# Chunk-selected attention feeding a soft mixture of experts: load order, score groups, slot steps and output halves rearranged in one change

## The chip, the cores and the metric

The kernel runs on one core of one Trainium2 chip. The metric is the time of one execution on the device in microseconds. The core has five engines that run their own instruction streams in program order: TensorE (PE in the profile, with its weight loads as PEld), VectorE (DVE), ScalarE (ACT), GpSimd (POOL) and SyncE (SP). Engines wait for each other through semaphores. Here GpSimd issues all loads and SyncE all stores.

## What is computed

The first part is attention in which every query sees only the six best chunks of 32 keys, chosen by an upper bound of the scores; the second part is a soft mixture of experts on the attention's output.

```python
# attention: B, H, S, D = 4, 8, 768, 64; chunk = 32, so 24 chunks; top_k = 6
k_min, k_max = k_chunks.min(axis=3), k_chunks.max(axis=3)
ub = sum over d of max(q * k_min, q * k_max)          # one bound per query and chunk
ub = where(causal by chunk, ub, -1e9)
top_chunks = argsort(ub)[..., -6:]
scores = q @ k.T / 8, kept where the chunk is selected and the key is not later
x = softmax(scores) @ v                               # to [3072, 512]

# soft MoE: 8 experts with 4 slots each, D = 512, F = 1024
logits = x @ phi
d = softmax of logits over the 3072 rows              # dispatch
slot_input = d.T @ x
slot_out[e] = relu(slot_input[e] @ w1[e]) @ w2[e]
c = softmax of logits over the 32 slots               # combine
out = c @ slot_out                                    # float32 [3072, 512]
```

Inputs come in float32 and are cast to bf16 by the load itself.

## The kernel before

The 32 heads are worked on in 16 pairs; the two heads of a pair share the 128 partitions, 64 each. The order of all work is written out by hand: a loop over slots `i` (lines 479 to 566) has for each slot a list of steps of different pairs, so that every engine finds work. In slot `i` these belong to pair `i`: `scores` and `expo` for six groups; to pair `i + 1`: the upper bound (`ubound`), the choice of chunks (`select`) and its transposes (`ns_transposes`, `evac_ns`); to pair `i + 2`: the transposes of k and q (`transposes`, `evac_T`), the chunk minima and maxima (`kmin`, `kmax`) and the split of q in its negative and positive part (`qsplit`); to pair `i - 1`: the product with v (`pv`); to pair `i - 2`: `normalise` and the transposes of x. The head is slots -2 and -1 of the same loop.

Scores are kept transposed (keys in partitions, queries along the row). A group is a list of pieces `(key block, first query offset, width, column)`; the causal triangle of 6 x 6 blocks of 128 is packed into six groups (line 30), three 512 and three 384 wide, for two heads at a time. Each piece costs two matmuls of keys against queries (line 270, one for each head) and two or four that add the mask of chunks which were not selected (line 280). ScalarE takes the exponential of a whole group (line 293), then GpSimd zeroes the upper triangle of the diagonal block (line 295). PSUM tiles come from three pools: `p_sc` (two, scores), `p_at` (one) and `p_tp` (two, everything else). A step whose tile isn't free yet makes TensorE wait, and with it all that stands behind on TensorE.

The mixture of experts runs batch by batch in slots behind the attention of that batch (`moe(step, i - 3)` does a step for the batch whose last pair is `i - 3`): `moe_logits`, `moe_copy`, `moe_max`, `moe_bound`, `moe_exp`, `moe_exp2`, `moe_scale`, `moe_comb`, `moe_comb2`, `moe_dispatch`, `moe_ct`. A running maximum lets the sums over rows be rescaled. The last batch is worked on behind the loop.

Loads go through one queue, in the order in which GpSimd issues them: k and q of pair `i + 4` (line 129) and v of pair `i + 2` (line 134), 192 KB each, and the sixteen expert weights (line 122), 1024 KB each, `w_sb[0..7]` for w1 and `w_sb[8..15]` for w2. `wplan` says how many weights a slot issues. Before, weight 0 is issued in the head, weight 1 in slot -1, and one in each slot from 2 to 15. Slots below 14 issue them behind `load_v`, slots 14 and 15 at their top.

Behind the loop come the last batch's dispatch, the first expert layer (`experts_in`, line 670, reads `w_sb[0..7]`), the second (`experts_out`, line 710) and the output. Experts are worked on in two groups `g` of four, four column tiles of TensorE at a time; `experts_out` for `g = 1` reads `w_sb[12..15]`, all four within the first four matmuls:

```python
def experts_out(f, gs, ys):
    for y, g in ((y, g) for y in ys for g in gs):
        for fg in range(f * 4, (f + 1) * 4):
            for j in range(4):
                e = g * 4 + j
                nc.tensor.matmul(so_ps[y][j * CH:(j + 1) * CH, :], lhsT=hT_pad[:, fg, e, :],
                    rhs=w_sb[E + e][:, fg * Dm + y * HD:fg * Dm + (y + 1) * HD], ...)
```

The output is 24 blocks of 128 rows, two to a store (line 761), scaled by VectorE and ScalarE by turns (lines 754 and 756). `keep(n)` issues n matmuls whose result isn't used.

Of the kernel before, what the change touches and what calls it, by code (L numbers as in the profile page):

```python
# [30 lines left out]
    [(0, 0, 384, 0)],  # L31
    [(1, 0, 256, 0), (0, 384, 128, 256)],
    [(2, 0, 512, 0)],
    [(5, 0, 128, 0), (1, 256, 384, 128)],
    [(3, 0, 384, 0)],
    [(4, 0, 256, 0), (0, 512, 256, 256)],
]
WIDTH = [sum(p[2] for p in g) for g in GROUPS]
BLOCK = {}
for _g, _pieces in enumerate(GROUPS):  # L40
    for _kg, _q0, _w, _c in _pieces:
        for _x in range(0, _w, P):
            BLOCK[(_kg, _kg + (_q0 + _x) // P)] = (_g, _c + _x)


@with_exitstack
def kernel(
# [41 lines left out]
    w_sb = []  # L89
    for i in range(EARLY):  # L90
        w_sb.append(static.tile([P, NDG * F], BF16, name=f"w_sb{i}"))
# [47 lines left out]

    load(0, "k")  # L140
    load(0, "q")
    make_identity(nc, ident)
    load(1, "k")
    load(1, "q")
    for t in (caus, qgrp, headsel, squad, ns_t[0], ns_t[1], c_pad):
        nc.vector.memset(t, 0.0)
    nc.vector.memset(ones_sq, 1.0)
    for t in v_t:
        nc.vector.memset(t[:, :, :, D:D + 1], 1.0)
    for h in range(2):  # L150
        nc.vector.memset(headsel[h * 64:(h + 1) * 64, :, h, :], 1.0)

    nc.gpsimd.affine_select(
# [9 lines left out]
    load_w(0)  # L163
    nc.gpsimd.affine_select(
        out=squad, in_=squad, compare_op=ALU.not_equal, fill=NEG, base=0,
        pattern=[[-CH, 2], [-64, 2], [-1, NCHUNK]], channel_multiplier=1,
    )
    nc.gpsimd.affine_select(
        out=squad, in_=squad, compare_op=ALU.not_equal, fill=-1.0, base=-NCHUNK,
        pattern=[[-CH, 2], [-64, 2], [0, NCHUNK]], channel_multiplier=1,  # L170
    )
    load_v(0)
    load_v(1)
# [38 lines left out]
    def qsplit(i):  # L212
        qT = st["qT", i]
        t = tpu.tile([P, 2, S], BF16, name="qpn", tag="qpn")
        nc.vector.tensor_scalar_min(t[:, 0, :], qT, 0.0)
        nc.vector.tensor_scalar_max(t[:, 1, :], qT, 0.0)  # L216
        st["qpn", i] = t
# [45 lines left out]
    def scores(i, g):  # L263
        ps = p_sc.tile([P, 2, 512], F32, name="sc_ps", tag="sc")
        kT, qT, nsT = st["kT", i], st["qT", i], st["nsT", i]
        for kg, q0, w, c in GROUPS[g]:
            qs = slice(kg * P + q0, kg * P + q0 + w)
            for h in range(2):
                r = slice(h * 64, (h + 1) * 64)
                nc.tensor.matmul(  # L270
                    ps[:, h, c:c + w], lhsT=kT[r, kg * P:(kg + 1) * P], rhs=qT[r, qs],
                    start=True, stop=False,
                )
            t0, t1 = kg + q0 // P, kg + (q0 + w) // P
            runs = [(x, max(t0, x * NJ), min(t1, (x + 1) * NJ)) for x in range(2)]
            runs = [r for r in runs if r[1] < r[2]]
            for x, f, l in runs:
                for h in range(2):
                    r = slice(h * 64, (h + 1) * 64)
                    nc.tensor.matmul(  # L280
                        ps[:, h, c + (f - t0) * P:c + (l - t0) * P],
                        lhsT=smask[r, x, kg].rearrange("p a b -> p (a b)"),
                        rhs=nsT[r, (f - x * NJ) * P:(l - x * NJ) * P], start=False, stop=(l == t1),
                    )
        st["scps", i, g] = ps

    def expo(i, g):
        w = WIDTH[g]
        if w == 512:
            e = ep.tile([P, 2, 512], BF16, name="e_sb", tag="e_sb")  # L290
        else:
            e = ep3.tile([P, 2, 384], BF16, name="e3_sb", tag="e3_sb")
        nc.scalar.activation(e[:, :, :w], st.pop(("scps", i, g))[:, :, :w], func=ACT.Exp, scale=scale)  # L293

        nc.gpsimd.affine_select(  # L295
            out=e[:, :, :P], in_=e[:, :, :P], compare_op=ALU.is_ge, fill=0.0,
            base=0, pattern=[[0, 2], [1, P]], channel_multiplier=-1,
        )
        st["e", i, g] = e

    def pv(i, ts):
# [7 lines left out]
        for t in ts:  # L309
            for h in range(2):  # L310
                o = at[:, h, (t - tb) * (D + 1):(t - tb + 1) * (D + 1)]
                for kg in range(t + 1):
                    g, c = BLOCK[(kg, t)]
# [68 lines left out]
    def moe_exp(b):  # L382
        lg = st["lg", b]
# [32 lines left out]
    def moe_comb(b):  # L416

        lg = st.pop(("lg", b))
# [31 lines left out]
    def moe_ct(b):  # L450
# [5 lines left out]
        nc.vector.tensor_copy(cT_all[:, b * NQT:(b + 1) * NQT, :], ps)  # L456
# [11 lines left out]
    wplan = {i: 1 for i in range(-1, NPAIR)}  # L468
    for i in (0, 1):
        wplan[i] = 0  # L470
# [8 lines left out]
    for i in range(-2, NPAIR):  # L479
# [4 lines left out]
        if have(i):  # L484
            scores(i, 0)
            expo(i, 0)
            scores(i, 1)
            expo(i, 1)
        moe(moe_max, i - 3)
        if have(i + 1):  # L490
            ubound(i + 1)
        if have(i - 2):
            normalise(i - 2)
        moe(moe_bound, i - 3)
        if have(i + 1):
            select(i + 1)
        if i == -1:
            nc.gpsimd.dma_start(out=phi_sb, in_=moe_phi.rearrange("(hg p) s -> p hg s", p=P))
            make_identity(nc, identf)
# [3 lines left out]
        if i == -1:  # L503
            ns_transposes(0)
            evac_ns(0)
        if have(i + 4) and i >= -1:
# [4 lines left out]
        moe(moe_exp, i - 3)  # L511
        if have(i):
# [4 lines left out]
        moe(moe_exp2, i - 3)  # L517
# [4 lines left out]
        if have(i + 2):  # L522
            transposes(i + 2, "q")
            evac_T(i + 2, "q")
            kmin(i + 2)
        if have(i - 2):
            evac_x(i - 2)
        if have(i + 2):
            kmax(i + 2)
        moe(moe_scale, i - 3)  # L530
        moe(moe_comb, i - 3)
        if have(i + 2) and i >= 0:
# [3 lines left out]
        if have(i):  # L536
            scores(i, 4)
            expo(i, 4)
            if i == LAST:
                pv(i - 1, [5])  # L540
            scores(i, 5)
            expo(i, 5)
        moe(moe_comb2, i - 3)
        if have(i + 1) and i >= 0:
            ns_transposes(i + 1)
            evac_ns(i + 1)
# [3 lines left out]
        if have(i - 1) and i < LAST:  # L550
            pv(i - 1, [5])
        if have(i + 2):
            qsplit(i + 2)
        if i == -2:
            nc.vector.tensor_tensor(schunk[:, :, :, 0], squad[:, :, 0, :], squad[:, :, 1, :], op=ALU.add)
            nc.scalar.copy(
                smask.rearrange("p o t a x -> p (o t a) x"),
                schunk.rearrange("p o c x -> p (o c) x").broadcast_to([P, 2 * NCHUNK, CH]),
            )
# [52 lines left out]
    keep(2)  # L612
# [12 lines left out]
    nc.vector.tensor_reduce(rm, lg1, axis=AX.X, op=ALU.max)  # L625
    dm = small.tile([P, 1, NS], F32, name="dm", tag="dm")
# [13 lines left out]
    op = ctx.enter_context(tc.tile_pool(name="op", bufs=5))  # L640
# [17 lines left out]
    cinv = tail.tile([P, B * NQT], F32, name="cinv")  # L658
    zinv = tail.tile([P, 1], F32, name="zinv")
# [28 lines left out]
    def zsum():  # L688
        ps = p_tp.tile([P, 1], F32, name="z_ps", tag="tp")
        nc.tensor.matmul(  # L690
            ps, lhsT=zrow.rearrange("p j s -> p (j s)"), rhs=identf[:1, :1], start=True, stop=True)
        nc.vector.reciprocal(zinv, ps)

    def csums():
        ps = p_tp.tile([P, B * NQT], F32, name="cs_ps", tag="tp")
        for n in range(B * NQT):
            nc.tensor.matmul(
                ps[:, n:n + 1], lhsT=cT[:, n // 2, n % 2], rhs=ones_sq[:, :1], start=True, stop=True)
        nc.vector.reciprocal(cinv, ps)

    HD = Dm // 2
    so_t = p_at.tile([P, 2, 512], F32, name="so_ps", tag="at")
    so_ps = [so_t[:, y, :HD] for y in range(2)]
# [20 lines left out]
    experts_out(0, [0], [0, 1])  # L724
    hidden_T(1)
    zsum()
    experts_out(0, [1], [0, 1])
    experts_out(1, [0, 1], [0])
    nc.scalar.activation(so_sb[0], so_ps[0], func=ACT.Copy, scale=zinv)
    experts_out(1, [0, 1], [1])  # L730
    nc.scalar.activation(so_sb[1], so_ps[1], func=ACT.Copy, scale=zinv)
    csums()


    homes = ((p_sc, "sc"), (p_tp, "tp"), (p_sc, "sc"), (p_tp, "tp"), (p_at, "at"))
    n = 0
    for m in range(B * NQT // 2):
        o_sb = op.tile([P, 2, Dm], F32, name="o_sb", tag="o_sb")
        rows = out[m * 2 * P:(m + 1) * 2 * P, :].rearrange("(p x) d -> p x d", x=2)
        for x in range(2):  # L740
            pool, tag = homes[n % 5]
            if n == 0:
                o_ps = pool.tile([P, 2, Dm], F32, name="o2_ps", tag=tag)
                halves = [o_ps[:, y, :HD] for y in range(2)]
            else:
                o_ps = pool.tile([P, Dm], F32, name="o_ps", tag=tag)
                halves = [o_ps[:, y * HD:(y + 1) * HD] for y in range(2)]
            for y in range(2):
                nc.tensor.matmul(halves[y], lhsT=cT[:, m, x], rhs=so_sb[y], start=True, stop=True)  # L749
            if n == 0:  # L750
                for y in range(2):
                    nc.vector.tensor_scalar_mul(o_sb[:, x, y * HD:(y + 1) * HD], halves[y], cinv[:, n:n + 1])
            elif x == 0:
                nc.vector.tensor_scalar_mul(o_sb[:, x, :], o_ps, cinv[:, n:n + 1])
            else:
                nc.scalar.activation(o_sb[:, x, :], o_ps, func=ACT.Copy, scale=cinv[:, n:n + 1])  # L756
            n += 1
            if m in (0, B * NQT // 2 - 1):
                nc.sync.dma_start(out=rows[:, x], in_=o_sb[:, x, :])
        if m not in (0, B * NQT // 2 - 1):  # L760
            nc.sync.dma_start(out=rows, in_=o_sb)
# [30 lines left out]
```

## Time and profile before

| what | value |
|---|---|
| median of three runs | 171.62 us (171.58 to 172.8) |
| the profiled execution | 172.21 us |
| its span, first to last instruction | 170.5 us |
| TensorE busy | 137.8 us (81%) |
| TensorE weight loads busy | 99.3 us (58%) |
| VectorE busy | 121.5 us (71%) |
| ScalarE busy | 122.6 us (72%) |
| GpSimd busy | 104.0 us (61%) |
| loads written by the software queue | 26.25 MB |
| stores by the hardware queue | 6.29 MB |
| first exponential of slot 0 | at 14.20 us |
| first exponential of slot 13 | at 110.79 us |
| first store issued | at 151.73 us |

The profile shows one execution. Its rows count from the first instruction; a time of day such as "at 110.79" is on that scale. Busy time is the union of an engine's instructions; TensorE's matmuls overlap and their ends are modelled, so its busy time says less than that of the others. The execution takes 1.7 us more than the span. In the 40 slices each slice is 4.26 us long, and its digits are tenths.

### The profile page before, as it was taken

The numbers are of one execution on the slowest core, as the hardware profiler recorded it, in microseconds if no ns is written. First come the engines' busy times: TensorE is split into PE (matmuls) and PEld (weight loads), VectorE is DVE, ScalarE is ACT, GpSimd is POOL, SyncE is SP. The second block draws the span as 40 slices with busy tenths as digits, with TensorE's granted clock in tenths as the row PEclk, the third lists the DMA queues.
The fourth block names the chain that finished last, engine by engine and source line by source line (L and its number), as shares of the span: only waits on it lengthen the run. The fifth ranks groups of instructions, "written<-read, shape, count | busy, mean of one in ns | idle before, by whom it ended". The sixth has DMA issues, their size and how long they took to land.

```text
span 170.5 us, 6183 instructions
## 1 busy us (share of the span) xinstructions
PE 137.8 (81%) x2574; PEld 99.3 (58%) x2575; DVE 121.5 (71%) x416; ACT 122.6 (72%) x166; POOL 104.0 (61%) x202
## 2 busy tenths in 40 slices
PE   0458988999999898999999899979889989896300
PEld 0335555777666767766776667657566855763200
DVE  3468768999999976999997798988742651166510
ACT  3355999999999877999987799978777522175510
POOL 7977759788878777888878878547663800000000
PEclk9999999999999999999999999999999999999965
DMA  3999999999999999999999999999999980029995
GB/s 46 163 156 185 182 212 188 129 152 184 184 214 190 211 197 209 193 211 195 212 197 205 196 207 202 203 203 200 202 208 212 215 163 13 4 76 407 404 400 195
DMA packets 40460, 32.94 MB, mean 193 GB/s; under 512 B 26352, under 2 KB 34544, under 8 KB 40432
## 3 DMA queue, kind: packets, MB, share of 16 engines
q0 software_dynamic: 38416, 26.25, 104.2%
q1 hardware_dynamic: 2016, 6.29, 9.4%
q8 instruction: 20, 0.33, 0.7%
q14 instruction: 8, 0.07, 0.1%
HBM read 52.49 MB, written 6.29 MB: 345 GB/s over the span
## 4 chain that ended last, share of the span: by engine, by line
PE 39%; ACT 21%; DVE 15%; DMA 14%; issue 5%; POOL 2%; DVEq 0%; ACTq 0%; POOLq 0%
ACT e_sb L293 15%; DMA k_in<-in_k_dram 10%; PE sc_ps L270 7%; PE at_ps L314 5%; PE tr_ps L181 5%; PE sc_ps L280 5%; DMA out_dram<-o_sb 4%; DVE x_sb L327 3%; PE h_ps L670 2%; PE so_ps L710 2%; DVE qpn L216 2%; PE ub_ps L229 2%; DVE mx L241 2%; ACT qT L190 2%; PE xT_ps L336 2%
## 5 line engine op out<-in xcount | busy, mean ns | idle before, releaser
L293 ACT ACTIVATE e_sb<-sc_ps 128x768 bf16<-128x768 f32 (+1 forms) x96 | 82.9, 930 | 9.7 <-PE sc_ps L280 9.7
L295 POOL TENSOR_SCALAR_AFFINE_SELECT e_sb<-e_sb 128x256 bf16<-128x256 bf16 x96 | 38.7, 413 | 19.6 <-ACT e_sb L293 18.9
L270 PE MATMUL sc_ps<-qT,kT 64*128 64x384 bf16 (+3 forms) x288 | 40.3, 299 | 4.2 <-ACT e_sb L293 4.1
L280 PE MATMUL sc_ps<-nsT,smask 64*128 64x384 bf16 (+2 forms) x320 | 38.6, 281 | 0.0
L314 PE MATMUL at_ps<-v_t,e_sb 128*128 128x65 bf16 x672 | 29.8, 194 | 1.5 <-DVE x_sb L327 1.2
L314 PEld LDWEIGHTS <-e_sb 128*128 128x128 bf16 x672 | 25.3, 98 | 3.9 <-DVE x_sb L327 1.2
L270 PEld LDWEIGHTS <-kT 64*128 64x128 bf16 x288 | 17.0, 95 | 15.5 <-issue 10.4
L241 DVE MAX8 mx<-ub_ps 128x8 f32<-128x8 f32 (+1 forms) x192 | 16.9, 161 | 3.6 <-PE ub_ps L229 2.0
L280 PEld LDWEIGHTS <-smask 64*128 64x128 bf16 x320 | 16.6, 96 | 3.8 <-issue 0.6
L199 DVE TENSOR_REDUCE mm<-kT 128x24 bf16<-128x768 bf16 x16 | 15.1, 945 | 4.6 <-ACT kT L190 4.5
L190 ACT COPY kT<-tr_ps 128x768 bf16<-128x768 bf16 x16 | 12.8, 799 | 7.5 <-PE tr_ps L181 6.7
L134 POOL DMA_DIRECT2D v_t<-in_v_dram x16 | 16.7, 1045 | 2.0 <-PE ns_ps L252 1.4
L327 DVE TENSOR_TENSOR x_sb<-at_ps,inv 128x768 bf16<-128x768 f32 (+1 forms) x17 | 15.5, 911 | 0.6
L205 DVE TENSOR_REDUCE mm<-kT 128x24 bf16<-128x768 bf16 x16 | 15.1, 943 | 0.0
L181 PE MATMUL tr_ps<-ident,k_in 128*64 128x128 bf16 x192 | 9.4, 240 | 6.3 <-DMA k_in<-in_k_dram 5.5
L190 ACT COPY qT<-tr_ps 128x768 bf16<-128x768 bf16 x16 | 12.9, 805 | 2.0 <-PE tr_ps L181 2.0
L129 POOL DMA_DIRECT2D k_in<-in_k_dram x16 | 11.7, 729 | 1.5 <-POOLq L776 0.8
L122 POOL DMA_DIRECT2D w_sb<-in_moe_w_dram x16 | 11.4, 710 | 1.5 <-DMA w_sb<-in_moe_w_dram 1.5
L756 ACT ACTIVATE o_sb<-o_ps,cinv 128x512 f32<-128x512 f32 x12 | 8.1, 686 | 4.9 <-PE o_ps L749 2.4
L129 POOL DMA_DIRECT2D q_in<-in_q_dram x16 | 11.5, 720 | 0.0
L216 DVE TENSOR_SCALAR qpn<-qT 128x768 bf16<-128x768 bf16 x16 | 11.0, 685 | 0.0
L347 DVE COPY xT_sb<-xT_ps 128x768 bf16<-128x768 bf16 (+1 forms) x15 | 8.1, 540 | 4.0 <-PE xT_ps L336 3.9
(116 smaller groups left out, 196.5 us busy)
## 6 DMA issues: line engine op xcount, KB each, us to landing
w_sb<-in_moe_w_dram POOLq DMA_DIRECT2D x16, 1024.0 KB, 14.4
out_dram<-o_sb SPq DMA_DIRECT2D x10, 512.0 KB, 4.9
k_in<-in_k_dram POOLq DMA_DIRECT2D x16, 192.0 KB, 9.7
q_in<-in_q_dram POOLq DMA_DIRECT2D x16, 192.0 KB, 10.0
v_t<-in_v_dram POOLq DMA_DIRECT2D x16, 192.0 KB, 10.8
out_dram<-o_sb SPq DMA_DIRECT2D x4, 256.0 KB, 3.4
phi_sb<-in_moe_phi_dram POOLq DMA_DIRECT2D x1, 32.0 KB, 9.0
```

What stands on the lines that cost most here:

```text
L129: nc.gpsimd.dma_start(out=t, in_=src.rearrange("h (p g) d -> p h (g d)", p=P))
L134: nc.gpsimd.dma_start(out=v_t[i % NV][:, :, :, :D], in_=v[b, 2 * j:2 * j + 2].rearrange("h (g p) d -> p h g d", p=P),)
L181: nc.tensor.matmul(ps[h * 64:(h + 1) * 64, g, :], lhsT=src[:, h, g * D:(g + 1) * D], rhs=ident, is_transpose=True,)
L190: nc.scalar.copy(t.rearrange("d (p g) -> d p g", g=NQT), st.pop((nm + "ps", i)).rearrange("d g p -> d p g"),)
L199: nc.vector.tensor_reduce(mm[:, 0, 0, :], kT, axis=AX.X, op=ALU.min)
L241: nc.vector.max(mx[:, a, :], ub[:, a, :max(8, 4 * t + 4)])
L270: nc.tensor.matmul(ps[:, h, c:c + w], lhsT=kT[r, kg * P:(kg + 1) * P], rhs=qT[r, qs], start=True, stop=False,)
L280: nc.tensor.matmul(ps[:, h, c + (f - t0) * P:c + (l - t0) * P], lhsT=smask[r, x, kg].rearrange("p a b -> p (a b)"), rhs=nsT[r, (f - x * NJ ...
L293: nc.scalar.activation(e[:, :, :w], st.pop(("scps", i, g))[:, :, :w], func=ACT.Exp, scale=scale)
L295: nc.gpsimd.affine_select(out=e[:, :, :P], in_=e[:, :, :P], compare_op=ALU.is_ge, fill=0.0, base=0, pattern=[[0, 2], [1, P]], channel_mult ...
L314: nc.tensor.matmul(o, lhsT=st["e", i, g][:, h, c:c + P], rhs=v_t[i % NV][:, h, kg, :], start=(kg == 0), stop=(kg == t),)
L327: nc.vector.tensor_tensor(st["x", b][:, t0:t1, 2 * j:2 * j + 2, :].rearrange("p t h d -> p h t d"), at[:, :, :, :D], inv.broadcast_to([P, ...
```

## The change

It has seven parts.

1. `GROUPS`: the two groups with 512 columns stand first, the pieces of key blocks 0 and 1 are dealt differently (eight pieces instead of nine), and the last pair has an order of its own, `GROUPS_LAST`. `expo` masks each piece that begins on the diagonal; there are six such blocks as before, with two in group 4 and none in group 5.
2. The head is written out ahead of the loop: eight matmuls on `ones_sq` into an unused tile first, then the first k; one, three and four more of them later. The mask tile `smask` is built first, the second k is transposed ahead of the first `ubound`, the positive part of the first q is taken by ScalarE, and weight 0 is issued last.
3. In slots 0 and 1 four groups are done in a row.
4. In each slot the MoE steps move: `moe_max` between groups 0 and 1, `moe_bound` ahead of `normalise`, `moe_comb` behind `select`, `moe_exp` behind groups 2 and 3, `moe_exp2` behind the q transposes; the copy of batch 2's combine weights moves to the last slot.
5. `wplan`: one weight in slots 2, 4, 5, 6, 8, 9, 10 and 12, two in 13, three in 14 and two in 15. The first eight weight tiles have a pool of their own that is closed ahead of the output, whose tiles take the room.
6. The column sums of the first three batches move ahead of the last batch's dispatch, where two spare matmuls stood; those of the last one join the row sum in `sums`.
7. The second expert layer is done one column half at a time, and the first six output blocks are computed, scaled and stored by halves.

```diff
 GROUPS = [
-    [(0, 0, 384, 0)],
-    [(1, 0, 256, 0), (0, 384, 128, 256)],
     [(2, 0, 512, 0)],
     [(5, 0, 128, 0), (1, 256, 384, 128)],
+    [(0, 0, 384, 0)],
     [(3, 0, 384, 0)],
-    [(4, 0, 256, 0), (0, 512, 256, 256)],
+    [(4, 0, 256, 0), (1, 0, 256, 256)],
+    [(0, 384, 384, 0)],
 ]
+GROUPS_LAST = [
+    [(0, 0, 512, 0)],
+    [(1, 0, 512, 0)],
+    [(2, 0, 384, 0)],
+    [(4, 0, 256, 0), (2, 384, 128, 256)],
+    [(3, 0, 384, 0), (1, 512, 128, 384)],
+    [(5, 0, 128, 0), (0, 512, 256, 128)],
+]
...
+    def warm(n):
+        r = ones_sq.rearrange("p (o c) -> p o c", o=1).broadcast_to([P, 4, P])
+        for _ in range(n):
+            nc.tensor.matmul(warm_ps, lhsT=ones_sq, rhs=r, start=True, stop=True)
...
-        nc.vector.tensor_scalar_max(t[:, 1, :], qT, 0.0)
+        if i == 0:
+            nc.scalar.activation(t[:, 1, :], qT, func=ACT.Relu)
+        else:
+            nc.vector.tensor_scalar_max(t[:, 1, :], qT, 0.0)
...
-    wplan = {i: 1 for i in range(-1, NPAIR)}
-    for i in (0, 1):
-        wplan[i] = 0
+    wplan = {i: 1 for i in (2, 4, 5, 6, 8, 9, 10, 12)}
+    wplan.update({13: 2, 14: 3, 15: 2})
...
-    for i in range(-2, NPAIR):
+    warm(8)
+    transposes(0, "k")
+    evac_T(0, "k")
+    kmin(0)
+    kmax(0)
+    warm(1)
+    transposes(0, "q")
+    evac_T(0, "q")
+    qsplit(0)
+    transposes(1, "k")
+    evac_T(1, "k")
+    warm(3)
+    ubound(0)
+    load(3, "k")
+    load(3, "q")
+    load_v(0)
+    transposes(1, "q")
+    evac_T(1, "q")
+    select(0)
+    load_v(1)
+    warm(4)
+    ns_transposes(0)
+    evac_ns(0)
+    kmin(1)
+    kmax(1)
+    qsplit(1)
+    nc.gpsimd.dma_start(out=phi_sb, in_=moe_phi.rearrange("(hg p) s -> p hg s", p=P))
+    make_identity(nc, identf)
+    load_w(0)
+
+    for i in range(NPAIR):
...
             scores(i, 0)
             expo(i, 0)
+        moe(moe_max, i - 3)
+        if have(i):
             scores(i, 1)
             expo(i, 1)
-        moe(moe_max, i - 3)
+        if i < 2:
+            scores(i, 2)
+            expo(i, 2)
+            scores(i, 3)
+            expo(i, 3)
         if have(i + 1):
             ubound(i + 1)
+        moe(moe_bound, i - 3)
         if have(i - 2):
             normalise(i - 2)
-        moe(moe_bound, i - 3)
+        if i == LAST:
+            moe_ct_copy(B - 2)
         if have(i + 1):
             select(i + 1)
...
+        moe(moe_comb, i - 3)
...
-        moe(moe_exp, i - 3)
-        if have(i):
+        if i >= 2:
             scores(i, 2)
             expo(i, 2)
             scores(i, 3)
             expo(i, 3)
-        moe(moe_exp2, i - 3)
+        moe(moe_exp, i - 3)
...
-    keep(2)
+    csa = p_tp.tile([P, BL * NQT], F32, name="cs_ps", tag="tp")
+    for b in range(BL):
+        col_sums(csa[:, b * NQT:(b + 1) * NQT], b)
...
-    experts_out(0, [0], [0, 1])
+    w_ctx.close()
+    op = ctx.enter_context(tc.tile_pool(name="op", bufs=5))
+    experts_out(0, [0, 1], [0])
     hidden_T(1)
-    zsum()
-    experts_out(0, [1], [0, 1])
+    sums()
+    experts_out(0, [0], [1])
     experts_out(1, [0, 1], [0])
     nc.scalar.activation(so_sb[0], so_ps[0], func=ACT.Copy, scale=zinv)
+    experts_out(0, [1], [1])
+    half_out(0, 0)
+    half_out(1, 0)
     experts_out(1, [0, 1], [1])
     nc.scalar.activation(so_sb[1], so_ps[1], func=ACT.Copy, scale=zinv)
-    csums()
+    half_out(2, 0)
+    for m in range(NH):
+        half_out(m, 1)
```

`half_out(m, y)` multiplies the two row blocks of `m` with column half `y`, scales one on VectorE and one on ScalarE and stores 256 columns of both rows; blocks from `m = 3` on are done as before.

## The prediction

> **What bounds the kernel now.** I read the 40 slices of the page first, then busy time by stretch, then the instructions in order of time for the loads, the slots and the tail.
>
> ```profile
> PEclk9999999999999999999999999999999999999965
> DMA  3999999999999999999999999999999980029995
> GB/s 46 163 156 185 182 212 188 129 152 184 184 214 190 211 197 209 193 211 195 212 197 205 196 207 202 203 203 200 202 208 212 215 163 13 4 76 407 404 400 195
> ```
>
> The transfers are busy from the first microseconds to about 140 us. No slice ahead of the output passes 215 GB/s (bytes written, bf16), so that is the rate at which loads arrive. Loads and compute are level: next come the stretches of slots 1 to 4, 5 to 8 and 9 to 12 (a slot runs from its first exponential to the next slot's) and the end of the loads.
>
> ```profile
> 22.35:49.82 27.47, 25.86 (x498) 18.59 (x498) 24.26 (x85) 26.04 (x34) 21.52 (x41) 1.00 1.32 178
> 49.82:80.28 30.46, 28.41 (x567) 21.16 (x567) 27.17 (x96) 26.88 (x37) 24.46 (x48) 1.00 1.35 201
> 80.28:110.79 30.51, 28.34 (x567) 21.17 (x567) 26.78 (x93) 27.01 (x38) 23.96 (x47) 1.00 1.31 203
> ...
> 127.00:139.00 12.00, 10.54 (x207) 7.78 (x205) 6.09 (x17) 7.16 (x11) 5.21 (x9) 1.00 1.04 210
> 139.00:143.00 4.00, 3.63 (x77) 1.90 (x73) 1.30 (x6) 0.88 (x3) 0.00 (x0) 1.00 0.30 61
> ```
>
> The fourth number after the length is ScalarE's busy time, the third VectorE's: both are busy some 88 to 95% of each stretch, so the slots have 1.4 to 3.6 us of slack per stretch and no more. The last column is the load rate: 210 GB/s while only weights are left.
>
> ```profile
> 110.20 0.70 POOL L122 DMA_DIRECT2D w_sb<-in_moe_w_dram  x1
> 117.83 0.70 POOL L122 DMA_DIRECT2D w_sb<-in_moe_w_dram  x1
> 119.29 0.72 POOL L122 DMA_DIRECT2D w_sb<-in_moe_w_dram  x1
> 125.95 0.77 POOL L122 DMA_DIRECT2D w_sb<-in_moe_w_dram  x1
> ```
>
> ```profile
> w_sb<-in_moe_w_dram POOLq DMA_DIRECT2D x1, 1024.0 KB, 17.0
> ```
>
> The last weight is issued at 125.95 and takes 17.0 us to land (transfers of that stretch): 142.95. It is one of the four that the second half of `experts_out` reads.
>
> ```profile
> 144.42 1.05 PE L710 MATMUL so_ps<-w_sb,hT_pad 128*32 128x256 bf16 x32
> ...
> 146.05 1.93 PE L710 MATMUL so_ps<-w_sb,hT_pad 128*32 128x256 bf16 x64
> ...
> 151.73 0.84 SPq L759 DMA_DIRECT2D out_dram<-o_sb  x2
> ```
>
> Group 1 (weights 12 to 15) is first read at 146.05, 3.1 us after the landing: no wait today, but only that much room. From there 24.4 us are left to the end of the span.
>
> **The change, part by part.** The span is 170.5 us, the profiled execution 172.21, the median of the runs 171.62; I work in the span and put its difference on the median.
>
> **Head.** The spare matmuls are to raise the clock early. The same shape costs 0.50 us ahead of 20 us and 0.34 behind it:
>
> ```profile
> 13.34 0.50 PE L270 MATMUL sc_ps<-qT,kT 64*128 64x384 bf16 x2
> ...
> 28.62 0.34 PE L270 MATMUL sc_ps<-qT,kT 64*128 64x384 bf16 x2
> ```
>
> Eight 512-column matmuls at about 0.43 (an estimate: the 512-column pair at 17.17 us is followed 0.40 later) fill 1.1 to 4.7 us, while PE waits for k anyway until 4.85. The mask copy (1.47 on ScalarE) now ends about 5.8, just ahead of the first kT copy; it costs nothing there, and 1.5 us if its POOL selects (0.32 and 0.28) come late. The second k stands ahead of the first bounds and lands near 7.7, not 7.49, since those selects precede its issue. ReLU on ScalarE takes one 0.87 us pass from VectorE. The bounds end near 9.5 instead of 10.41, the first exponential starts near 12.5 instead of 14.20. Slot 0 then does four groups in a row: 2 x 0.91 + 2 x 0.75, then kT 0.80, qT 0.80 and two more groups, 6.7 us against 8.15. Slot 1 starts near **19.3** instead of 22.35. If the clock stays low, the spare matmuls (one, three and four at 0.43) stand in the path and the gain is about 0.4: from 0.4 to 3.0, I take 3.0 because the first stretch of PE becomes gapless.
>
> The Trainium skill, "TensorE: Matmul & The Clock Gate", Part 1, says that one busy window of about 3.4 us raises the clock and one idle window halves it. By that the eight are just enough here; no row shows it yet.
>
> **Slots.** Groups with 1024 elements stand first: 0.3 us more cover for the 0.22 us wait in front of the third group. Eight pieces instead of nine save two score and two mask matmuls (about 0.1 us of PE, which isn't the bound); the causal selects stay six a slot. `moe_bound` ahead of `normalise` and `moe_exp` behind two groups take away the 1.04 us gap of slots 6 and 10 (kT's transposes waiting for `mb`). The gap of 1.10 behind `moe_ct` stays. I give slots 1 to 4 27.1 (from 27.47), the two stretches with MoE 29.2 each (from 30.46 and 30.51), between no gain and ScalarE's busy sum. Slot 13 starts at 19.3 + 27.1 + 29.2 + 29.2 = 104.8; its weights are issued 6.3 later, as in slot 12 (103.93 to 110.20), because k for pair 15, which came 12.76 us after its issue, is no longer queued behind weights: **111.1** instead of 117.83.
>
> **Late weights.** Only weights 0 to 8 are issued before that point; nine to fifteen are still to go: 7 x 1.049 MB = 7.34 MB. At 210 GB/s that is 35.0 us. In slots 1, 3 and 7 the queue has only k, q and v (0.59 MB, about 3.5 us of a 6.8 us slot), so it runs dry there and this time isn't recovered. Ahead of it is a rest of v, 0.6. The slowest of the engines ends later: at 139 us 61 GB/s x 4 us = 0.24 MB were left, worth 1.2 us at full rate, yet the landing was at 142.95, 2.8 later. Landing of weight 15: 111.1 + 0.6 + 35.0 + 2.8 = **149.5**. Bounds: 34.1 at 215 GB/s without the lag, 38 at 203 with it.
>
> POOL issues three at the top of slot 14 (3 x 0.70) and two in slot 15; behind them wait the selects, needed a slot later, so 2.1 us are covered (and cost that much otherwise).
>
> Compute would be ready at 111.1 + (144.42 - 117.83) + 0.3 - 1.0 = 137.0 (16 matmuls of group 0 first; slots 14 and 15 give up about 1 us of their gaps). So PE stands about **12.5 us** in `experts_out(0, [0, 1], [0])`. Behind that matmul on PE stand `hidden_T(1)`, `sums`, every other expert matmul and all output matmuls; for those wait ScalarE, VectorE and SP.
>
> **Tail.** Column sums of three batches replace two `keep` matmuls (18 of some 0.03 = 0.5 against 0.4): nothing. The first output goes out behind one column half: from the wait's end 16 + 16 + 32 matmuls and 16 more beside the 0.48 scaling. Warm (32 in 0.87 to 1.05), with transposes, sums, scaling and o_sb, that is about 4.0 us to the first issue; cold, twice the PE part, about 6.1. The clock went down in the last slices, some 2 us behind the last matmul, so behind 12 idle microseconds I take cold at first, 5.6. Today issue to span end is 18.8, at 404 GB/s; halves leave the queue short for about 0.8 while the other half is computed, so 19.4. Together 25.0 (22.6 to 26.5), against 24.4 today.
>
> By the same section's window rule the clock would be back about 3.4 us into the tail; 5.6 would be nearer 5.2, and the sum 0.4 lower.
>
> **Sum.** 149.5 + 25.0 = 174.5 us of span, +4.0: **175.6** against the median 171.62. Gained: 3.0 head, 2.9 slots, 0.8 the late k, 1.0 in slots 14 and 15, and 1.3 because group 1 is now asked for 0.3 behind group 0 instead of 1.6; spent: 12.5 of waiting and 0.6 in the tail.
>
> **Rivals.**
> *The slots fall to ScalarE's sum* (other side). With the queue free and no waits, slots 1 to 12 could take 26.04 + 26.88 + 27.01 = 79.9, not 85.5: weights issued at 105.5, span 105.5 + 0.6 + 35.0 + 2.8 + 25.0 = 168.9, time **170.0**. It decides from slots at or below 81.5 (then it is no slower than before). For it: the order is rid of two kinds of wait. Against: VectorE needs 78.2 too, and chains run through both.
> *The weights arrive in time.* Without the wait: 171.62 - 7.7 - 1.6 (output halves first) = **162.3**. For it: landings of weights among other loads are some 4.6 us apart. Against: 7.34 MB in 26 us is 282 GB/s, and no load slice passes 215.
> *The clock stays low in the head.* Spare matmuls delay instead: 2.6 us later everywhere, **178.2**. For it: before, the clock was low for 15 us of fairly dense matmuls.
>
> **Chances.** Forecast 0.69 (0.06 of it within 1%), low clock 0.08, slots at the floor 0.16 (0.10 within 1%, 0.06 better with a warm tail), weights in time 0.07. So faster by over 1% (about what a measurement tells from nothing) 0.13, within 0.16, slower 0.71. The bounds of the terms (issue 109 to 113, stream 37 to 40, tail 22.6 to 26.5) spread the forecast itself from 172 to 179; the range takes in the floor rival: 169.0 to 179.0.
>
> **What would show it.** Right: matmuls of 64x384 near 0.34 by 13 us; slot 1 near 19.3; weight 9 issued near 111; the last weight landing near 149 and an idle PE of 10 us or more in front of the second expert group; slow matmuls behind it; first output issue near 155. Wrong: no wait there (rate above 220 GB/s or slots far shorter), or load slices busy in slots 1 to 7 as before.

## The result and the profile after

| what | before | after |
|---|---|---|
| median of four runs each | 171.83 us (171.58 to 172.8) | **183.26 us** (181.13 to 183.72) |
| ratio to before | | 1.063, 95% interval 1.0536 to 1.0723 |
| the profiled execution | 172.21 us | 183.72 us |
| its span | 170.5 us | 182.0 us |
| first exponential of slots 1 and 13 | 22.35, 110.79 | 20.65, 108.40 |
| first weight of slot 13 issued | 117.83 | 114.16 |
| last weight issued, landed | 125.95, 142.95 | 124.10, 153.89 |
| second expert group, first matmul behind the last weight | 146.05 | 153.93 |
| first store issued | 151.73 | 160.72 |

The change makes the kernel 6.3% slower; forecast were 175.6 us and at most 179.0. Here and below, medians are over all executions, while ratios leave out those that ran in a slower state, so the two can differ by a per cent.

The slices of the page of after (clock in tenths, bytes written; 4.55 us each):

```profile
PEclk9879999999999999999978999999996975579855
...
GB/s 50 155 144 167 200 95 129 114 188 177 134 206 191 213 192 209 171 170 198 201 193 203 183 29 199 169 200 216 214 215 215 213 212 81 4 115 330 405 404 133
```

The queue runs low in four places: slices 6 to 8 (95 to 129), 11 (134), 17 and 18 (about 170) and 24 (29, at 104.6 to 109.2 us, just ahead of the seven late weights). From slice 28 on it is full, at 212 to 216, up to 150 us. What was not fetched in the low slices is fetched behind everything else.

Busy time by stretch of after: slots 1 to 4, 5 to 8, 9 to 12; then, behind a row left out, from 139.00 (within the first expert layer) to the last landing; from there to the first store; the stores. Columns: window, length, busy PE, PEld, DVE, ACT, POOL with instructions, granted clock, DMA share, GB/s.

```profile
20.65:48.00 27.35, 25.71 (x482) 17.99 (x482) 24.70 (x88) 25.97 (x33) 21.16 (x42) 1.00 1.19 144
48.00:77.52 29.52, 28.01 (x551) 20.26 (x551) 27.02 (x95) 26.79 (x37) 24.08 (x46) 1.00 1.34 192
77.52:108.40 30.88, 29.38 (x551) 20.86 (x551) 27.60 (x97) 27.11 (x38) 23.08 (x47) 0.94 1.21 170
...
139.00:153.90 14.90, 5.36 (x73) 2.27 (x72) 0.85 (x3) 1.19 (x2) 0.00 (x0) 0.73 0.92 184
153.90:160.70 6.80, 6.77 (x97) 4.43 (x97) 1.04 (x5) 0.81 (x2) 0.00 (x0) 0.50 0.01 2
160.70:182.00 21.30, 8.34 (x77) 5.24 (x76) 8.41 (x14) 8.46 (x16) 0.00 (x0) 0.74 0.78 297
```

Slots 1 to 4 loaded at 178 GB/s before and at 144 now. In the row from 139.00 PE is busy for 5.36 of 14.90 us, most of it in the first expert layer; in the next, which leads to the first store, its clock is 0.50 throughout.

The chain that ended last, and PE's matmuls of the second expert layer in order of time (start, duration, what; in brackets the idle time before it and who ended it):

```profile
124.10 29.79 DMA w_sb<-in_moe_w_dram
```

```profile
143.01 0.71 PE L781 MATMUL so_ps<-w_sb,hT_pad 128*32 128x256 bf16 x17
144.20 0.27 PE L781 MATMUL so_ps<-w_sb,hT_pad 128*32 128x256 bf16 x1 [0.48 <-DMA w_sb<-in_moe_w_dram]
149.04 0.37 PE L781 MATMUL so_ps<-w_sb,hT_pad 128*32 128x256 bf16 x1 [4.57 <-DMA w_sb<-in_moe_w_dram]
153.93 1.01 PE L781 MATMUL so_ps<-w_sb,hT_pad 128*32 128x256 bf16 x13 [4.52 <-DMA w_sb<-in_moe_w_dram]
...
156.18 3.61 PE L781 MATMUL so_ps<-w_sb,hT_pad 128*32 128x256 bf16 x64
```

Group 0 runs through. Group 1 waits for the last three weights, one after the other: 0.48, 4.57 and 4.52, 9.6 us together. The last issue took 29.79 us to land, against 17.0 before. Behind the wait 64 matmuls take 3.61 us; 64 of the same shape took 1.93 before.

Against before, the second group starts 7.88 us later (146.05 to 153.93), and from there to the end of the span it takes 28.1 instead of 24.4. Together that is the 11.5 us.

### The profile page after: what moved, and what is told of

The parts are those of the page before. It is cut to its first block, busy times and chain, and to the rows that moved or that the text cites. A ratio compares the mean times of both kernels' runs of the same rounds, so it can differ in the third digit from the quotient of the medians.

```text
span 182.0 us, 6100 instructions
## 1 busy us (share of the span) xinstructions
PE 146.6 (81%) x2532; PEld 99.3 (55%) x2533; DVE 120.0 (66%) x417; ACT 123.5 (68%) x170; POOL 103.9 (57%) x202
## 4 chain that ended last, share of the span: by engine, by line
PE 27%; DMA 21%; ACT 21%; DVE 11%; POOL 10%; issue 6%; SPq 1%; POOLq 0%; DVEq 0%; ACTq 0%
DMA w_sb<-in_moe_w_dram 16%; ACT e_sb L321 13%; PE sc_ps L297 4%; PE sc_ps L307 3%; PE so_ps L781 3%; POOL e_sb L325 3%; PE tr_ps L205 3%; DMA out_dram<-o_sb 3%; PE at_ps L344 3%; ACT qT L214 3%; DVE mx L268 2%; POOL w_sb L138 2%; DMA k_in<-in_k_dram 2%; DVE x_sb L357 2%; PE ub_ps L256 2%
## 5 line engine op out<-in xcount | busy, mean ns | idle before, releaser
L321 ACT ACTIVATE e_sb<-sc_ps 128x1024 bf16<-128x1024 f32 (+1 forms) x96 | 82.9, 918 | 5.8 <-PE sc_ps L307 5.5
L325 POOL TENSOR_SCALAR_AFFINE_SELECT e_sb<-e_sb 128x256 bf16<-128x256 bf16 x96 | 39.2, 425 | 21.0 <-ACT e_sb L321 20.6
L297 PE MATMUL sc_ps<-qT,kT 64*128 64x384 bf16 (+3 forms) x258 | 37.2, 310 | 3.9 <-ACT e_sb L321 3.2
L297 PEld LDWEIGHTS <-kT 64*128 64x128 bf16 x258 | 14.3, 94 | 12.3 <-issue 7.3
L307 PEld LDWEIGHTS <-smask 64*128 64x128 bf16 x294 | 15.2, 96 | 4.2 <-issue 1.3
L781 PE MATMUL so_ps<-w_sb,hT_pad 128*32 128x256 bf16 x128 | 7.4, 375 | 9.6 <-DMA w_sb<-in_moe_w_dram 9.6
L145 POOL DMA_DIRECT2D q_in<-in_q_dram x16 | 11.5, 722 | 0.0
L781 PEld LDWEIGHTS <-hT_pad 128*32 128x32 bf16 x128 | 4.5, 129 | 11.9 <-issue 10.7
L764 DVE COPY hT_pad<-hT_ps 128x64 bf16<-128x64 bf16 x4 | 0.6, 188 | 15.5 <-PE hT_ps L760 15.5
L827 ACT ACTIVATE so_sb<-so_ps,inv_b 128x256 bf16<-128x256 f32 x1 | 0.5, 474 | 15.2 <-PE so_ps L781 15.2
```

What stands on the lines that cost most here:

```text
L145: nc.gpsimd.dma_start(out=t, in_=src.rearrange("h (p g) d -> p h (g d)", p=P))
L297: nc.tensor.matmul(ps[:, h, c:c + w], lhsT=kT[r, kg * P:(kg + 1) * P], rhs=qT[r, qs], start=True, stop=False,)
L307: nc.tensor.matmul(ps[:, h, c + (f - t0) * P:c + (l - t0) * P], lhsT=smask[r, x, kg].rearrange("p a b -> p (a b)"), rhs=nsT[r, (f - x * NJ ...
L325: nc.gpsimd.affine_select(out=e[:, :, c:c + P], in_=e[:, :, c:c + P], compare_op=ALU.is_ge, fill=0.0, base=0, pattern=[[0, 2], [1, P]], ch ...
```

## The experiments

**Theory A**: the late weights hold up the second expert layer, and everything else in the change is worth a few us of gain. **The rivals**: the head, the slot order or the output halves cost the time themselves; or the low clock behind the wait does. Each kernel ran beside the kernel before on the same chip.

### Weights spread evenly, the rest of the change kept

```diff
-    wplan = {i: 1 for i in (2, 4, 5, 6, 8, 9, 10, 12)}
-    wplan.update({13: 2, 14: 3, 15: 2})
+    wplan = {i: 1 for i in range(1, NPAIR)}
```

> The changed kernel with one weight in each slot from 1 to 15 instead of seven in the last three. Theory A (the deferred weights cost the time: 10.6 us of waiting in the second expert layer and 3 us of a slow clock behind it): the last weight lands before 143, no wait, span 168 to 170, time near 170. Theory B (the reordered head, slots and halves are slow in themselves, and the wait only hides that): time stays above 175. If the queue runs late again, k of pair 15 comes about 1 us late in slot 13.

Measured: 174.11 us (172.72 to 175.81), ratio 1.0163 (1.0082 to 1.0243). The last weight landed at 142.04 and the second layer, begun at 145.43, waited for none. So nine of the eleven us are the plan. But it is still slower than before, between what the two theories expected. The trace shows where: GpSimd stood 9.8 us in front of weight issues until earlier weights had landed, and PE waited 3.7 us for k.

```profile
POOL w_sb L138 <- DMA w_sb<-in_moe_w_dram: 9.8, 6, 3.0
...
PE tr_ps L205 <- DMA k_in<-in_k_dram: 3.7, 3, 1.9
```

(Waits between 30 and 120 us: sum, times, longest.) Slots 9 and 12 took 8.57 and 9.95 us, where 7.1 and 6.5 are usual; in slot 12 the clock was also at 0.5 from 104.9 to 108.3. That it is the weight in slot 1, ahead of the k of later pairs, which fills the queue too early was argued and not shown.

### The plan alone, on the kernel before

```diff
-    wplan = {i: 1 for i in range(-1, NPAIR)}
-    for i in (0, 1):
-        wplan[i] = 0
+    wplan = {i: 1 for i in (2, 4, 5, 6, 8, 9, 10, 12)}
+    wplan.update({13: 2, 14: 3, 15: 2})
```

> The kernel before with the new plan of weights and nothing else. Theory A: the weights of slot 13 are issued near 116.7 (k of pair 15 no longer late), the last one lands 39.7 later as in the changed kernel, 156.4; from there the old tail takes 24.4 warm and 26 to 27 at a low clock: span 182 to 183.5, time 183 to 185, so more than the whole loss of the change. Theory B: the plan alone costs a few us at most, time under 176.

Measured: 185.91 us (183.67 to 188.21), ratio 1.0735 (1.064 to 1.0829). The plan alone costs all of the loss and more. Its second layer in order of time (here line 709):

```profile
155.57 0.37 PE L709 MATMUL so_ps<-w_sb,hT_pad 128*32 128x256 bf16 x1 [4.49 <-DMA w_sb<-in_moe_w_dram]
160.47 3.57 PE L709 MATMUL so_ps<-w_sb,hT_pad 128*32 128x256 bf16 x61 [4.52 <-DMA w_sb<-in_moe_w_dram]
```

The same two gaps, 6.5 us later than in after. Slot 13's weights were issued 5.5 later, at 119.67 instead of the expected 116.7: slot 10 took 12.00 us in this execution, the longest of the four (188.21). The matmuls behind them are slow here too, so that is the wait's doing and not the halves'.

### Nothing to wait for: weights 12 to 15 not loaded

```diff
-            load_w(nw)
+            if nw < E + 4:
+                load_w(nw)
...
-                        rhs=w_sb[E + e][...],
+                        rhs=w_sb[E + j][...],
```

Experts 4 to 7 use the second-layer weights of experts 0 to 3.

> The changed kernel in which experts 4 to 7 use the second-layer weights of experts 0 to 3, so that weights 12 to 15 are neither loaded nor waited for (this part of the computation is changed). Theory A: the second layer runs through from 143, the clock stays up, first store near 148, span 167 to 168, time near 169. Theory B: time above 175. It leaves the first 114 us as they are and so prices wait and slow tail together: 13 to 15 us.

Measured: 166.72 us (166.29 and 167.16), ratio 0.97 (0.9625 to 0.9774), span 165.4. The second layer began at 139.86 and the first store came at 144.66, 4.80 later; in after it came 6.83 behind the last landing, although 19 of that half's 64 matmuls were done by then. Without the wait the rest of the change gains 3%, with 4 MB less to load. The theory holds, and of the first rival nothing is left as a net cost.

### The clock kept up through the wait

```diff
-    experts_out(0, [0, 1], [0])
+    experts_out(0, [0], [0])
+    spare = p_tp.tile([P, 512], F32, name="spare_ps", tag="tp")
+    for _ in range(48):
+        nc.tensor.matmul(spare, lhsT=ident, rhs=w_sb[E][:, :512], start=True, stop=True)
+    experts_out(0, [1], [0])
```

> The changed kernel with 48 spare matmuls (0.216 us each, 10.4 us) between the first and the second expert group, where TensorE otherwise stands idle. The last weight still lands near 154. If the slow clock behind the wait costs what the prediction's cold tail says and more, the first store comes 4.5 instead of 6.8 behind the landing and the time falls by 2 to 3.5 us, to about 180. If the tail is long because of the column halves or the store queue, it stays at 183.

Measured: 183.18 us (180.36 to 185.25), with no ratio on record; the expected fall to about 180 is not in the median. In the profiled execution the head ran 2.64 us later than after's (first exponential at 15.93 instead of 13.29), so the whole can't show the term. The trace does. PE of this kernel, and the stretch from landing to first store:

```profile
157.67 1.93 PE L781 MATMUL so_ps<-w_sb,hT_pad 128*32 128x256 bf16 x64
```

```profile
156.20:160.60 4.40, 4.20 (x105) 3.40 (x108) 1.04 (x5) 0.91 (x3) 0.00 (x0) 1.00 0.00 0
```

With the clock at 1.00 the 64 matmuls take 1.93 us, as before, and the first store comes 4.40 behind the landing instead of 6.83. From landing to end the tail takes 25.3 us instead of 28.1, in one execution each. So 2.8 us of the tail are the clock that the wait lets fall. That the execution as a whole gains them was not shown.

### The weights early, where the queue runs low

```diff
-    wplan = {i: 1 for i in (2, 4, 5, 6, 8, 9, 10, 12)}
-    wplan.update({13: 2, 14: 3, 15: 2})
+    wplan = {i: 1 for i in range(2, NPAIR) if i != 6}
+    wplan[0] = 2
```

> The changed kernel with the weights as early as k can bear: two in slot 0 (where the queue ran dry at 95 to 130 GB/s), none in slots 1 and 6, one in each other slot to 15. Theory A (the load queue bounds the kernel: it has to be busy from the start and still bring k in time): no wait in the second expert layer, k late by under 2 us in all (3.3 us of idle ScalarE in slot 12 with one weight a slot from slot 1), span 167 to 169, time 168 to 171. Theory B (a queue that is always full makes k late whatever the order): slots 9 to 13 again 4 us longer than without the last weights, time 173 to 175.

Measured: 169.91 us (168.84 to 171.43), ratio 0.9859 (0.9811 to 0.9907). The last weight landed at 140.42, and the second layer ran without a wait:

```profile
143.21 1.05 PE L781 MATMUL so_ps<-w_sb,hT_pad 128*32 128x256 bf16 x32
...
145.08 1.93 PE L781 MATMUL so_ps<-w_sb,hT_pad 128*32 128x256 bf16 x64
```

With only `wplan` different from after, 13.3 us less (183.26 - 169.91): the cost of the late weights, with all that hangs on it. With this plan the whole is 1.4% faster than the kernel before. How much of that is the plan and how much the other six parts is open: the early plan was not tried on the kernel before, and with a weight in every slot the same six parts were 1.6% slower than it.

### Two steps further in the slots

In after, slots 6 and 10 took 9.40 and 10.26 us, where they took 9.46 and 9.57 before. The wait that the moved steps took away is gone; another stands there. GpSimd of after in slot 6, and ScalarE's wait for it:

```profile
59.03 0.74 POOL L145 DMA_DIRECT2D k_in<-in_k_dram  x1
59.77 0.72 POOL L145 DMA_DIRECT2D q_in<-in_q_dram  x1
60.50 0.78 POOL L325 TENSOR_SCALAR_AFFINE_SELECT e_sb<-e_sb 128x256 bf16<-128x256 bf16 x2
61.24 0.60 POOL L424 TENSOR_TENSOR ld<-lg,m_run 128x192 f32<-128x192 f32 x1
```

```profile
61.88 0.36 ACT L436 ACTIVATE d_sb<-ld 128x192 bf16<-128x192 f32 x1 [1.43 <-POOL ld L424]
```

`ld`, which `moe_exp` needs, stands behind two load issues and two selects on GpSimd. The edit, on top of the early plan, for slots 6, 10 and 14:

```diff
-        if have(i + 4):
+        late = have(i - 3) and i % NPB == 2
+        if have(i + 4) and not late:
...
+        if have(i + 4) and late:
+            load(i + 4, "k")
+            load(i + 4, "q")
```

the second behind `moe(moe_exp, i - 3)`.

> The same, and in slots 6, 10 and 14 k and q of pair i + 4 are issued behind moe_exp instead of ahead of it. If GpSimd's order made slots 6 and 10 as long as before (9.4 to 9.5 us: ld stood behind two issues and two selects, and the exponential of ld waited 1.4 us for it), these slots fall to 8.2 to 8.6 each and the time by up to 2 us against the plan alone. If the chain through VectorE bounds them, they stay above 9.2.

Measured: 169.79 us (168.54 to 171.29), ratio 0.9861 (0.9831 to 0.989). Slots 6 and 10 fell to 8.04 and 8.15, as expected, yet slot 14 began at 116.16 as with the early plan alone (116.24). Slots 6 and 10 gained 2.8 us against the early plan alone; slots 7 and 11 gave back 1.5 of it, and slots 8 and 13 another 1.2. (This execution also began slot 1 0.9 earlier and lost that in slot 3.) In slots 3, 8 and 13 PE waited for k. The waits for k between 30 and 120 us, early plan alone first, then with the moved loads:

```profile
PE tr_ps L205 <- DMA k_in<-in_k_dram: 1.3, 2, 1.0
```

```profile
PE tr_ps L205 <- DMA k_in<-in_k_dram: 3.4, 3, 2.0
```

To see whether that is the queue, the same move was made where weights 12 to 15 are not loaded and the queue has room:

> The kernel without the last four weights (experts 4 to 7 use those of 0 to 3 in the second layer) and with k and q of slots 6, 10 and 14 issued behind moe_exp. Here the load queue has room. If the 1.4 us that this move saved in slots 6 and 10 was given back only because k came late behind weights, it now stays: slot 13 starts 2.5 to 3 us ahead of 106.9, time near 164. If it is lost to another wait in any case, the time stays at 166.7.

Measured: 167.95 us (165.07 to 168.51), no interval; span 163.4 against 165.4 with the same head (slot 1 at 20.21 in both). Slot 13 began at 105.40 instead of 106.94: 1.54 us of gain, less than expected, because slots 7 and 11 grew by 0.7 and 0.6. PE waits for VectorE there, 0.61 in each; in slot 7:

```profile
64.96 0.54 PE L344 MATMUL at_ps<-v_t,e_sb 128*128 128x65 bf16 x12 [0.61 <-DVE x_sb L357]
```

The kernel with all weights has the same waits, 0.55 and 0.60. So only the loss in slots 8 and 13 goes with late k; the one in slots 7 and 11 stands with room in the queue too. The gain itself is that of one execution, the fastest of four; the other three took 167.59 to 168.51.

### The spare matmuls taken out of the head

```diff
-        for _ in range(n):
+        for _ in range(0):
```

First on the kernel with the early plan and the moved loads:

> The kernel with loads behind moe_exp, without the sixteen spare matmuls of the head. If they raise the clock in time, the first exponential comes 1 to 1.5 us later than with them (near 14 instead of 12.5 to 13.3) and slot 1 begins near 22 instead of 20. If their gain hangs on where the clock's window falls (first exponentials of 12.5, 12.9, 13.3 and 15.9 so far, same code), the time without them lies within 1 us and scatters less.

Measured: 170.31 us (168.57 to 171.25), ratio 0.9869 (0.9826 to 0.9912). Slot 1 began at 22.70 instead of 20.15, and slot 14 at 116.34 instead of 116.16. Most of the lead was gone by slot 4 (43.05 against 43.53): with the spare matmuls, PE waited 1.97 us for k in slot 3. The same on the kernel without weights 12 to 15:

> The kernel without the last four weights, without the spare matmuls of the head. With all weights, leaving them out cost 2.5 us at slot 1 and nothing from slot 14 on. If that was the load queue again, here, where it has room, the delay stays: slot 13 starts near 109.5 instead of 106.9 and the time is 1.5 to 2.5 us above 166.7. If the spare matmuls are worth nothing, the time stays within 0.7.

Measured: 170.16 us (168.99 to 172.52), ratio 0.9874 (0.9815 to 0.9932) against 0.97 with them; slot 13 at 109.60 instead of 106.94. So by the times the spare matmuls are worth some 3 us where the queue has room, and nothing that shows where it is full. The trace bears out less: of the 2.66 us at slot 13, 0.92 are there at the start of slot 1. The rest came in slots 1, 10 and 11, where the clock of this execution was at 0.5 (23.1 to 26.5, 94.8 to 98.2) and that of the kernel with spare matmuls was not. Whether those stretches hang on the spare matmuls was not shown. Four kernels from 20 to 110 us (the last column is GB/s): early plan, moved loads, moved loads without spare matmuls, and the one without the last weights.

```profile
20.00:110.00 90.00, 83.20 (x1605) 59.14 (x1605) 79.98 (x280) 81.95 (x108) 72.13 (x139) 1.00 1.35 201
```

```profile
20.00:110.00 90.00, 82.93 (x1607) 59.09 (x1604) 79.68 (x286) 82.14 (x108) 71.53 (x139) 1.00 1.35 201
```

```profile
20.00:110.00 90.00, 85.87 (x1624) 60.45 (x1620) 80.55 (x281) 83.46 (x110) 72.77 (x141) 1.00 1.35 201
```

```profile
20.00:110.00 90.00, 84.88 (x1645) 60.44 (x1642) 81.82 (x293) 83.01 (x110) 70.34 (x138) 1.00 1.27 171
```

The first three load 201 GB/s whatever their head and slots do; the fourth needs only 171.

### Whole rows instead of halves

`NH = 0`, no `half_out`, the first block's two rows stored singly; on the kernel with the moved loads.

> The one before, with all output blocks as full rows (no column halves; the second expert layer keeps its order). The first store comes 1.0 to 1.6 us later, but from first store to the end of the span it takes 18.8 as in the kernel before instead of 20.8 to 21.3. If that holds, the halves gained nothing: time the same within 0.6 us. If the halves carry their gain of 1.3 to 1.6, this one is slower by that much.

Measured: 172.64 us (169.47 to 174.81), ratio 0.9881 (0.9825 to 0.9936); the profiled head was late (first exponential at 14.93). From the first matmul of the second layer to the end it took 25.69 us, and 25.59, 25.47 and 25.18 in the three kernels with halves. Halves bring the first store forward by 1.6 (6.39 to 4.81 behind that matmul), and the stores then take 20.8 instead of 19.3. By these single executions they gain 0.1 to 0.5, much less than the 1.6; the ratios don't tell the two apart.

### One more plan

`wplan = {i: 1 for i in range(NPAIR) if i not in (6, 10)}; wplan[13] = 2`, with the moved loads.

> The kernel with loads behind moe_exp, and one weight in slots 0, 1 to 5, 7 to 9, 11 and 12, two in slot 13, one in 14 and 15: ten instead of eleven ahead of k of pair 15, and no two at once in slot 0. If slot 14's start (116.2 in three kernels with different heads and MoE orders) is set by what the queue holds ahead of the last k, it moves to 113.5 to 115, the last weight lands at 139 to 140 as before, TensorE waits under 1 us for it, span 165 to 166, time 167 to 168.5: below both kernels. If the end of the queue is what counts, nothing is gained: 169.5 to 170.

Measured: 169.03 us (168.86 to 172.11), ratio 0.9853 (0.9804 to 0.9901). The expected earlier slot 14 did not come: 116.23, with one weight fewer ahead of the last k. PE waited for k in slots 6 and 8 (1.2 and 1.0 us) and not in slot 13. So what the queue holds ahead of the last k does not set this point, and why four kernels begin slot 14 within 0.2 us of each other stays open. The early plan alone, the one with the moved loads and this one lie within 1 us and can't be told apart; all three are about 1.4% below the kernel before.

## Why the prediction was right in kind and short in size

Right were the sign and the place: seven weights behind slot 13, a second expert group that waits for them, slow matmuls behind the wait. The sum gave a span of 174.5 us; it was 182.0. The 7.5 us between stand in three of its terms.

| term | forecast | measured | short by |
|---|---|---|---|
| issue of slot 13's first weight | 111.1 | 114.16 | 3.06 |
| from there to the last landing | 38.4 | 39.73 | 1.33 |
| from the landing to the end | 25.0 | 28.11 | 3.11 |

**Head: 1.35 of the 3.06.** Slot 1 was to start at 19.3 and started at 20.65. Two steps failed. The first is "the first stretch of PE becomes gapless". The eight matmuls did raise the clock at 4.4 us, but PE then waited for q and the second k, and the clock was low again from 7.8 to 11.2. PE of after from 8 us:

```profile
8.17 1.46 PE L197 MATMUL warm_ps<-ones_sq 128*128 128x512 bf16 x3
...
11.06 1.10 PE L197 MATMUL warm_ps<-ones_sq 128*128 128x512 bf16 x4
```

These seven stand in the path for 2.4 us, the first four at the low clock. The first exponential came at 13.29 instead of 12.5. In four kernels with the same head whose clock did not fall there it came at 12.49 to 12.86, so the fall cost about 0.4 to 0.8.

The second step is the 6.7 us for slot 0. It took 7.36, and 7.35 where the clock stayed up: the sum sets the copies of kT and qT back to back, and ScalarE waited 0.17 and 0.61 for their transposes.

```profile
16.81 0.80 ACT L214 COPY kT<-tr_ps 128x768 bf16<-128x768 bf16 x1 [0.17 <-PE tr_ps L205]
18.22 0.80 ACT L214 COPY qT<-tr_ps 128x768 bf16<-128x768 bf16 x1 [0.61 <-PE tr_ps L205]
```

The rival in which the spare matmuls only delay is not borne out: without them slot 1 started at 22.70 and 21.13, with them at 20.15 and 20.21 in the same two kernels. These are single executions, and with spare matmuls it also started as late as 22.40 and 23.28, where the second k came 1.7 and 1.9 us later than in after.

**Slots: 2.25 of it**, 0.25 in slots 1 to 4, 0.32 in 5 to 8 and 1.68 in 9 to 12; the weights being issued 5.76 instead of 6.3 into slot 13 gave 0.54 back. Plain slots fell from 6.87 to 6.51, with ScalarE idle for 0.04, but slot 1, with its four groups in a row, took 7.72. The step that failed is counting as time gained that the moved steps "take away the 1.04 us gap of slots 6 and 10". The gap is gone, but ScalarE then waited 1.43 for `ld`; GpSimd's load issues, which cost nothing in my sum, stand ahead of it. The rest is slot 10, 10.26 us where two other kernels, the same up to slot 13, took 9.52 and 6.66 for slots 10 and 11 against 10.26 and 6.95 here; in this execution, and not in theirs, PE's clock was at 0.5 from 93.1 to 96.5.

**Stream: 1.33.** The rate was right: seven landings 4.9 us apart, 214 GB/s. Ahead of them stood more than "a rest of v, 0.6": weight 8, issued at 107.65, landed at 116.40, 2.2 us behind the issue of the next. The prediction named slots 1, 3 and 7 as those in which the queue runs dry and left out slot 11, which has no weight either: the slice at 29 GB/s is the time until weight 8 was issued in slot 12.

**Tail: 3.11.** I had the low clock for part of the way. It lasted from 147.8 to 161.4, past the first store (6.8 instead of 5.6 behind the landing), and the stores took 21.3 instead of 19.4. The kernel that kept the clock up splits this: its tail is 25.3, 4.40 to the first store where I had 4.0, and 20.9 for the stores where I had 19.4. So 1.5 is missing in the stores, where I gave the halves 0.6 over before (with whole rows they took 19.3, so the halves cost some 1.6), 0.4 in the way to the first store, and the remaining 1.2 the clock, 2.8 instead of the 1.6 in my sum. The Trainium skill, "TensorE: Matmul & The Clock Gate", Part 1, has the clock back after one busy window of about 3.4 us, which I weighed and which would have made the forecast 0.4 shorter. The traces are divided. In after two whole windows with PE busy throughout, from 154.6, passed before the clock rose at 161.4; with the plan alone on the kernel before, one window from 160.7 to 164.1, with PE busy for 3.36 of 3.41 us, was enough.

**POOL's issues in slot 14** were put down as covered. Slot 14 took 8.51 us, and 8.15 in kernels with fewer weights issued at its top: 0.36, hidden under the landing here.

**The wait** was 9.6, not 12.5, because compute came 6.3 us later than forecast (the second layer at 143.01 instead of 136.7): 3.06 from the issue point, some 1.5 in slots 14 and 15, which were to gain 1.0 and lost 0.5, 0.2 in the last dispatch, and 1.6 in the first expert layer (6.05 us against 4.48; the clock was at 0.5 from 137.5 to 140.9). Group 0 took 0.7 instead of 0.3, two matmuls ran between the waits, and the last weight landed 4.4 later. None of it moves the end, since the landing does.

**The other rivals.** The slots did not fall to ScalarE's sum: 87.75 us for slots 1 to 12, where that rival needed 79.9, and still 85.2 with the queue free and `ld` moved. Weights in time would have given 162.3; the kernel that needn't wait took 166.7, so even without the wait I had the slots too short.

## What to carry to other kernels

Where loads fill the queue, the order and the total decide: a load that is put off is paid for behind the last one, and compute saved elsewhere can be lost again, here to waits for the next k and for VectorE. Before taking a wait away, read what stands in front of the next instruction on the engine that releases it. An idle stretch costs its own length and then the slow clock behind it; both belong in the sum.

## What the runs showed of the hardware

The granted clock changes on a grid of 3.4 us (in after at 4.40, 7.81 and 11.22; all later changes lie whole steps behind), and it fell behind windows in which PE was far from idle. Two windows of after, before the fall at 7.8 and behind it:

```profile
4.40:7.80 3.40, 1.83 (x34) 1.06 (x35) 1.30 (x2) 2.81 (x3) 3.40 (x7) 1.00 1.12 157
7.80:11.20 3.40, 3.40 (x41) 2.06 (x36) 1.86 (x14) 1.61 (x4) 2.37 (x3) 0.50 1.06 143
```

PE was busy for 1.83 of the 3.40 us; it was 2.10 ahead of the fall in slot 10 and 3.01 ahead of the one in the first expert layer. So a window need not be idle to lower it. PE's busy time alone does not tell, though: two other windows of after, from 14.6 and from 59.0 us, held 2.11 and 2.18 us of it, and the clock stayed up. What sets the threshold was not tested.

The Trainium skill, "TensorE: Matmul & The Clock Gate", Part 1, says that the windows run freely and don't begin with the kernel. The trace agrees: in nine kernels with the same head code the clock first rose at 4.24 to 7.17 us, by the trace's clock records, although the first matmul stood at 1.12 in all.

In these nine the first exponential came at 12.49 to 15.93 us. Where the clock did not fall again in the head it came by 12.86, with one low window that ended by 12.3 at 13.29 to 13.82. In the two latest, 14.93 and 15.93, the low clock lasted to 13.1 and 14.6, and the second k also came late (9.24 and 9.45 against 7.57 in after), so there the clock is not the only cause.
